# The end of a bias stage: merged stores, an early table load, and unread matmuls ahead of the first bias

## The chip, the core and the metric

The program runs on one core of one Trainium2 chip. The metric is the device time of one execution in microseconds (us), the lower the better. Before the change the median of 3 runs is 822.11 us (817.0 to 824.08). The core's engines are called by the profile's short names: PE (TensorE matmul), DVE (VectorE), ACT (ScalarE), POOL (GpSimd) and SP (SyncE, which here issues nearly all DMA transfers). The core has 16 DMA engines.

## The reference

Attention with a bias that a small network makes of the positions, and two feed-forward stages behind it. Cut to what matters:

```python
B, H, S, D = 4, 8, 576, 64
scores = (1 / sqrt(D)) * q @ k.T                       # per batch and head
x = log1p(|i - j|) / log1p(max(i, 1))                  # per pair of positions
bias = maximum(x[..., None] @ w1 + b1, 0) @ w2         # hidden 32, one value per head
attn = softmax(scores + bias[head])
x = (attn @ v)  as rows of 512
x = (g(x @ w_in)) @ w_out                              # 512 -> 2048 -> 512, g a leaky relu
out = soft mixture of 8 experts over x                 # 32 slots, experts 512 -> 1024 -> 512
```

The bias is the same for all 4 batches, so it is made once, at the start.

## The kernel before

**Stages.** The bias stage runs first (0 to about 75 us of the trace), then attention over 16 pairs of (two heads, one batch), then the feed-forward stage, then the experts. Each stage is one stream of instructions per engine, put in order when the kernel is built; instructions marked with `keep_in_program_order` keep their place, others are placed by the builder's scheduler. Once built, each engine runs its list in order, and a wait stops all that stands behind it.

**The bias stage** (`bias_phase`). The bias of one head depends on i and on |i - j|, so the kernel computes rows over the distance d = 0 to 575, in 9 steps `k` of 64 distances. In each step ACT and DVE make 16 masks (`make_mask`, L142 and L144) in a ring of `RING` buffers; PE reads all 16 for each row tile `c` (`unit`, L160); DVE combines two products into `rows` (L189, then L193 or L191); POOL writes the mirror image into the same tile (L211). The rows are split into row tiles c = 0 to 3 (two blocks of 64 positions each, one per half of the 128 partitions) and c = 4 (the middle block). Step k has the tiles c = 3 down to 0 as far as k <= 8 - c, and c = 4 for k < 5.

**Pieces and stores.** `CHUNKS[c]` cuts the steps of a row tile into pieces. A piece collects its steps in one SBUF tile `rows{c}_{i}`; with its last step it is sent to a scratch tensor in DRAM, `W` for c < 4 and `W4` for c = 4 (`send`, L216). Each half of the partitions goes out in DMAs of its own, 64 partitions each. The SBUF tiles are named by `TAGS`, one letter per piece; pieces with the same letter share a buffer, and the later one waits until the earlier one's stores have landed. With the last pieces only the first of four head pairs is sent at once (`flush(slice(0, 1))`), the other three at the very end (`late`).

**The first bias.** Attention reads the bias of a head pair back from `W` and `W4` into the tile `nb` (L345). For the first pair this goes in four parts: `att.bias_first(s)` for s = 0 to 3, part s needing row tile c = 3 - s, and the c = 4 block with s = 0. On SP the stores of the steps k > 4 and these loads stand in written order: the stores of step 6, then part 0, then the stores of step 7, part 1, the stores of step 8, parts 2 and 3, then the late stores. Behind them come the loads of the next pairs: `raw` (L365, q and k), `v` (L371), `wide` (L655, a weight of the feed-forward stage) and `nb` of the next head pair. SP hands its DMAs eight semaphores in turn, so a DMA is not issued before the one eight places ahead of it has landed.

**Attention's start.** Per pair and tile t: `scores` (S, PE L414) into PSUM, `least` (z, DVE L437: adds the bias, keeps the minimum), `power` (e, ACT L457: exp), `transposes` (T, PE L477), `gather` (g, L491 or L493), `pv` (P, PE L505). Nine tiles make a pair. The scores' PSUM pool has 4 buffers, so S of the tiles 0 to 3 of pair 0 can run before any bias is there, and S of tile 4 waits for z of tile 0. POOL splits q and k of each pair into high and low parts (L382, L384), two pairs ahead; between two of these splits the builder has put the first block of the feed-forward input (L633 to L635), which needs pair 0's result written to DRAM (`xT`, L518) and read back (`xu`, `xb`, L618, L622).

Of the kernel before, what the change touches and what calls it, by code (L numbers as in the profile page):

```python
# [13 lines left out]
AF = mybir.ActivationFunctionType  # L14
# [5 lines left out]
P = 128  # L20
# [15 lines left out]
NG = 9  # L36
NTQ = S // 4
PITCH = 2 * S
RING = 40
ACC = 4  # L40
CHUNKS = ((0, 2, 4, 7, 9), (0, 2, 4, 6, 8), (0, 3, 5, 7), (0, 2, 4, 6), (0, 2, 4, 5))
TAGS = ("cfgc", "becb", "gbd", "ada", "mnm")
LATE, EARLY = "bcdg", "aefmn"
ENGS = (
    "VVVAVVAVVAVVAVVA", "AAAVAAAVAAAVAAAV", "AAAVAAAVAAAVAAAV", "AAAVAAAVAAAVAAAV", "AAAVAAAVAAAVAAAV", "AAVAAVAAVAAVAAVA",
    "AAVAAVAAVAAVAAVA", "AVAAVAVAAVAVAAVA", "AVAVAVAAVAVAVAVA",
# [23 lines left out]
def bias_phase(tc, ident, W, W4, cpack, lcol, prow, xmain, xtail, att):  # L70


    nc = tc.nc
    with ExitStack() as ctx:
# [25 lines left out]
        sg = cp.tile([P, 4], F32, name="sg")  # L100
# [31 lines left out]

        mask = mp.tile([P, RING, S], BF16, name="mask")

        def make_mask(k, u):

            t = 16 * k + u
            n = min(S, 128 * (NG - k))
            dst = mask[:, t % RING, :n]
            on = ENGS[k][u]  # L140
            if on == "A":
                nc.scalar.activation(dst, pr[:, :n], AF.Sigmoid, bias=wb[:, t : t + 1], scale=BIG)  # L142
            else:
                nc.vector.tensor_scalar(dst, pr[:, :n], wl[:, t : t + 1], None, ALU.is_gt)  # L144
# [3 lines left out]
        def unit(k, c):  # L148
# [9 lines left out]
            for u in range(16):  # L158
                for part in range(3):
                    nc.tensor.matmul(  # L160
                        dst[:, u // 8, :, :, 4 * (u % 8) : 4 * (u % 8) + 4],
                        mask[:, (16 * k + u) % RING, cols],
                        wp[:, part],
# [3 lines left out]
            if c == 4 and k in (0, 2):  # L167
                return
            ks = CHUNKS[c]
            i = max(n for n in range(len(ks)) if ks[n] <= k)  # L170
# [6 lines left out]
            if f0 == 0:  # L177
                tag = TAGS[c][i]
                rows[c] = fps[tag].tile([P, H * 2 * w], F32, tag=tag, name=f"rows{c}_{i}")
# [84 lines left out]
        for k in range(NG):  # L264
            cs = [c for c in range(3, -1, -1) if k <= NG - 1 - c]
            if k < 5:
                cs.append(4)
            done = 0
            for n_, c in enumerate(cs):
                unit(k, c)  # L270
                if k + 1 < NG:
                    upto = 16 * (n_ + 1) // len(cs)
                    for u in range(done, upto):
                        make_mask(k + 1, u)
                    done = upto
            if k < 4:
                att.split(0, k)
            if k in (6, 7):
                att.bias_first(k - 6)
        att.load(1)  # L280
        att.load_v(1)
        att.bias_first(2)
# [5 lines left out]
class Attention:  # L288
# [107 lines left out]
    def scores(self, i, t):  # L396
        nc, st = self.nc, self.st[i]
        slot = self.SLOT[t]
        if slot == 0:
            st["sum"] = self.op.tile([P, 9], F32, tag="sum", name=f"sum{i}")  # L400
        s = self.ps.tile([P, 2, 512], F32, tag="p", name=f"s{i}_{t}")
        if slot < 4:
            terms = [(P * slot, 0)]
        elif slot == 4:
            terms = [(512, 0), (576, 1)]
        else:
            terms = [(704 + P * (slot - 5), 1)]
        seq = [(o, h, a, b) for o, h in terms for a, b in ((0, 0), (0, 1), (1, 0))]
        for n_, (o, h, a, b) in enumerate(seq):
            for hf in range(2):  # L410
                d = slice(64 * hf, 64 * hf + 64)
                self.pin(
                    i,
                    nc.tensor.matmul(  # L414
                        s[:, hf, :288],
                        st["q", a][d, o : o + P],
                        st["k", b][d, 288 * h : 288 * h + 288],
                        start=n_ == 0,
                        stop=n_ == len(seq) - 1,
                    ),  # L420
                )
        st["s", t] = s
# [738 lines left out]
def kernel(  # L1161
# [17 lines left out]
        for n, b in (("a_raw", 2), ("a_v", 3), ("a_split", 2))  # L1179
    )  # L1180
    bias_phase(tc, ident, W, W4, cpack, lcol, prow, xmain, xtail, att)

    kp = ctx.enter_context(tc.tile_pool(name="m_keep", bufs=1, reuse_waits="tile"))
# [167 lines left out]
```

## Time and profile before

| | before |
|---|---|
| median of 3 runs | 822.11 us |
| lowest and highest | 817.0 and 824.08 us |
| the profiled execution | 819.86 us |
| its span, first to last instruction | 817.8 us |
| mean granted TensorE clock in it | 0.974 of 2.4 GHz |

The span is what the trace covers; 2.06 us of the profiled execution lie around it. The views used below: busy time of each engine in chosen stretches, each engine's instructions in order of time with what ended its idle time, the chain of waits that ended last, and the DMA's traffic. A granted clock of 1.00 is 2.4 GHz and 0.50 is 1.2 GHz.

### The profile page before, as it was taken

What the parts mean: (1) busy time and instruction counts of PE and PEld (TensorE: products, weight loads), DVE (VectorE), ACT (ScalarE), POOL (GpSimd) and SP (SyncE); (2) the same over time, 40 slices, a digit from 0 to 9 for tenths busy, and PEclk for the clock granted to TensorE, in tenths of its full rate; (3) what the DMA queues carried; (4) which work ended last, traced back from release to release, by engine and by line L of the source; (5) the groups of instructions that cost most, each with busy time, mean ns of one, the idle gap of its engine ahead of it and who ended that gap; (6) DMA issues with size and microseconds to landing.
All of it is one profiled execution on the core that took longest, in us unless ns stands there. A gap on an engine that the chain in (4) does not pass through costs nothing.

```text
span 817.8 us, 18364 instructions
## 1 busy us (share of the span) xinstructions
PE 769.4 (94%) x7428; PEld 641.0 (78%) x7428; DVE 549.2 (67%) x958; ACT 495.7 (61%) x974; POOL 316.5 (39%) x239
## 2 busy tenths in 40 slices
PE   6886898999999999999999999999999999998993
PEld 6785776787877779988898889888999898885432
DVE  8896686888898866777668465646675756565003
ACT  8973786888888854443447566656666656554002
POOL 4632137365475712113224463454444451231000
PEclk9999798999999999999999999999999999998997
DMA  6599987729743442332330011301100134338996
GB/s 197 132 228 218 306 200 211 218 92 256 236 135 129 145 152 81 126 103 103 132 101 1 1 40 40 129 1 41 37 1 20 30 129 130 99 107 303 382 372 231
DMA packets 49669, 114.44 MB, mean 140 GB/s; under 512 B 10544, under 2 KB 29872, under 8 KB 47536
## 3 DMA queue, kind: packets, MB, share of 16 engines
q1 hardware_dynamic: 49584, 113.26, 44.5%
q8 instruction: 58, 0.95, 0.5%
q14 instruction: 27, 0.22, 0.1%
HBM read 91.95 MB, written 21.29 MB: 138 GB/s over the span
## 4 chain that ended last, share of the span: by engine, by line
PE 79%; DVE 6%; DMA 5%; issue 3%; POOL 3%; ACT 2%; SPq 1%; DVEq 0%; POOLq 0%; ACTq 0%
PE h L724 23%; PE ys L756 22%; PE o L505 9%; PE s L414 8%; PE t L477 4%; PE acc L160 4%; PE ops L1125 3%; PE hps L1125 2%; DMA xT<-xo 2%; DMA W<-rows 2%; DVE mask L144 1%; PE lp L816 1%; DMA em<-in_mw_dram 1%; SPq L345 1%; DVE rows L193 1%
## 5 line engine op out<-in xcount | busy, mean ns | idle before, releaser
L735 DVE SCALAR_TENSOR_TENSOR g<-g,nal 128x384 f32<-128x384 f32 x96 | 100.0, 1041 | 82.3 <-ACT g L734 82.2
L437 DVE CUSTOM_DVE_ANT_0 z<-s,nb 128x576 f32<-128x576 f32 x144 | 108.2, 755 | 24.5 <-PE s L414 14.0
L457 ACT ACTIVATE e<-z,m 128x576 f32<-128x576 f32 x144 | 109.9, 767 | 6.8 <-DVE m L437 6.8
L742 ACT ACTIVATE gr<-g 128x384 fp32r<-128x384 f32 x95 | 49.7, 523 | 86.3 <-DVE g L735 86.2
L493 ACT ACTIVATE g<-t 128x640 f32<-128x640 f32 x96 | 67.3, 703 | 35.4 <-PE t L477 31.4
L505 PE MATMUL o<-g,v 128*64 128x256 f32 (+1 forms) x640 | 86.3, 415 | 0.5 <-ACT g L493 0.5
L732 ACT ACTIVATE g<-h 128x384 f32<-128x384 f32 x96 | 46.9, 489 | 54.3 <-PE h L724 51.9
L744 DVE TENSOR_TENSOR gr<-g,gr 128x384 fp32r<-128x384 f32 x79 | 53.4, 677 | 33.7 <-ACT gr L742 30.4
L477 PE MATMUL t<-ident,e 64*128 64x64 f32 x1440 | 69.9, 227 | 3.8 <-DVE m L437 2.8
L477 PEld LDWEIGHTS t<-ident,e 64*128 64x128 f32 x1440 | 67.7, 143 | 5.3 <-issue 4.1
L160 PE MATMUL acc<-wp,mask 128*128 128x64 bf16 (+1 forms) x1680 | 57.2, 198 | 14.8 <-DVE rows L193 6.0
L160 PEld LDWEIGHTS <-mask 128*128 128x128 bf16 (+1 forms) x1680 | 55.1, 103 | 16.8 <-DVE rows L193 6.6
L414 PE MATMUL s<-kh,qh 64*128 64x288 f32 x320 | 62.5, 386 | 5.8 <-DVE m L437 4.0
L505 PEld LDWEIGHTS o<-g,v 128*64 128x64 f32 x640 | 43.8, 138 | 29.0 <-ACT g L493 1.0
L142 ACT ACTIVATE mask<-pr,wb 128x576 bf16<-128x576 f16 (+4 forms) x94 | 54.8, 678 | 6.3 <-PE acc L160 6.2
L414 PE MATMUL s<-kl,qh 64*128 64x288 f32 x320 | 49.1, 302 | 2.7 <-POOL kl L384 2.7
L744 POOL TENSOR_TENSOR gr<-g,gr 128x384 fp32r<-128x384 f32 x16 | 19.7, 1231 | 78.1 <-ACT gr L742 68.2
L414 PE MATMUL s<-kh,ql 64*128 64x288 f32 x320 | 49.1, 302 | 0.0
L382 POOL TENSOR_SCALAR qh<-raw 128x1216 fp32r<-128x1216 f32 x16 | 19.3, 1209 | 74.6 <-PE t L477 38.9
L734 ACT ACTIVATE g<-h 128x384 f32<-128x384 f32 x96 | 46.5, 485 | 0.0
L384 POOL TENSOR_TENSOR ql<-raw,qh 128x1216 fp32r<-128x1216 f32 x16 | 45.2, 2827 | 0.0
L414 PEld LDWEIGHTS s<-kh,qh 64*128 64x128 f32 x320 | 31.7, 194 | 14.9 <-DVE m L437 4.7
(986 smaller groups left out, 2020.2 us busy)
## 6 DMA issues: line engine op xcount, KB each, us to landing
wide<-in_w_dram SPq DMA_DIRECT2D x16, 1024.0 KB
ep<-in_mw_dram SPq DMA_DIRECT2D x30, 512.0 KB
raw<-in_qk_dram SPq DMA_DIRECT2D x16, 896.0 KB
nb<-W SPq DMA_DIRECT2D x6, 1152.0 KB
v<-in_v_l_dram SPq DMA_DIRECT2D x16, 320.0 KB
pre<-in_mw_dram SPq DMA_DIRECT2D x10, 512.0 KB
er<-in_mw_dram SPq DMA_DIRECT2D x9, 512.0 KB
em<-in_mw_dram SPq DMA_DIRECT2D x8, 512.0 KB
```

Source lines behind the costliest of these rows:

```text
L142: nc.scalar.activation(dst, pr[:, :n], AF.Sigmoid, bias=wb[:, t : t + 1], scale=BIG)
L160: nc.tensor.matmul(dst[:, u // 8, :, :, 4 * (u % 8) : 4 * (u % 8) + 4], mask[:, (16 * k + u) % RING, cols], wp[:, part], start=part == 0, ...
L414: nc.tensor.matmul(s[:, hf, :288], st["q", a][d, o : o + P], st["k", b][d, 288 * h : 288 * h + 288], start=n_ == 0, stop=n_ == len(seq) - 1,),
L437: self.nc.vector.tensor_tensor_reduce(out=z.rearrange("p (a b) -> p a b", a=2), in0=s[:, :, :288], in1=nb.rearrange("p (a b) -> p a b", a= ...
L457: self.nc.scalar.activation(e, z, AF.Exp, bias=m, scale=-1.0, accum_out=st["sum"][:, slot : slot + 1]),
L477: self.pin(i, nc.tensor.transpose(tp[:, r, 64 * c : 64 * c + 64], e[q, k0 : k0 + P], self.ident[q, q]))
L493: self.pin(i, nc.scalar.activation(dst, src, AF.Copy))
L505: nc.tensor.matmul(op[64 * h : 64 * h + 64, 0, :n], st["v"][:, h, c], g[:, h, c], start=c == 0, stop=c == 4),
L724: nc.tensor.matmul(h, w_[:, c * P : (c + 1) * P], x_[:, c], start=c == 0 and n_ == 0, stop=c == NC - 1 and n_ == 2,)
L735: nc.vector.scalar_tensor_tensor(g, neg, self.nal[:, f : f + 1], g, ALU.mult, ALU.add)
L744: eng.tensor_tensor(gl, g, gh.bitcast(F32), ALU.subtract)
L756: i = self.nc.tensor.matmul(self.ys[blk][t], g_[:, t * P : (t + 1) * P], w_[:, 512:], start=f == 0 and n_ == 0, stop=f == NF - 1 and n_ == 2,)
```

## The change

Four edits, all at or for the end of the bias stage.

1. **Pieces.** Row tile c = 1 goes out in three pieces (steps 0-1, 2-5, 6-7) instead of four (0-1, 2-3, 4-5, 6-7); row tile c = 3 in two (0-3, 4-5) instead of three (0-1, 2-3, 4-5). The letters change with it: the piece of steps 5-6 of c = 2 takes the letter f instead of d, and the letter f belongs to the piece of steps 2-3 of c = 0.
2. **Ring.** The ring of masks has 32 buffers instead of 40.
3. **Table.** One exp of a single column is run on ACT behind the last mask, so that the table of exponentials is loaded there.
4. **Matmuls.** 14 matmuls of 512 columns stand on PE ahead of the scores of tile 3 of pair 0, into the buffer of that tile; the scores then overwrite it.

```diff
-RING = 40
+RING = 32
 ACC = 4
-CHUNKS = ((0, 2, 4, 7, 9), (0, 2, 4, 6, 8), (0, 3, 5, 7), (0, 2, 4, 6), (0, 2, 4, 5))
-TAGS = ("cfgc", "becb", "gbd", "ada", "mnm")
-LATE, EARLY = "bcdg", "aefmn"
+CHUNKS = ((0, 2, 4, 7, 9), (0, 2, 6, 8), (0, 3, 5, 7), (0, 4, 6), (0, 2, 4, 5))
+TAGS = ("cfgc", "beb", "gbf", "ad", "mnm")
+LATE, EARLY = "bcfg", "ademn"
+WARM = 14
@@ bias_phase
             if k in (6, 7):
                 att.bias_first(k - 6)
+        tc.keep_in_program_order(nc.scalar.activation(sg[:, 3:4], ident[:, :1], AF.Exp))
         att.load(1)
@@ Attention.scores
+        if i == 0 and t == 3:
+            for _ in range(WARM):
+                self.tc.keep_in_program_order(
+                    nc.tensor.matmul(s[:, 0], st["q", 0][:, :P], st["k", 0][:, :512], start=True, stop=True)
+                )
```

How the built programs differ. First SP, the start of its stores (`rows3_0_207` is the first piece of row tile 3, the last number only counts; the shape is partitions x head pairs x float columns, so 64x4x510 are runs of 2,040 bytes in DRAM). Before:

```order
L216 DMA W_57<-rows3_0_207 64x4x510 x2
L216 DMA W4_58<-rows4_0_720 64x8x64 x2
L216 DMA W_57<-rows1_0_321 64x4x510 x2
L216 DMA W_57<-rows0_0_378 64x4x382 x2
L216 DMA W4_58<-rows4_0_720 64x8x63
L216 DMA W4_58<-rows4_0_720 64x8x64
L216 DMA W_57<-rows2_0_264 64x4x766 x2
L216 DMA W_57<-rows3_1_783 64x4x256 x4
L216 DMA W_57<-rows1_1_898 64x4x256 x2
L216 DMA W4_58<-rows4_1_1300 64x8x64
L216 DMA W_57<-rows0_1_955 64x4x256 x2
```

And SP in the changed program, the same place:

```order
L217 DMA W4_58<-rows4_0_718 64x8x64 x2
L217 DMA W_57<-rows1_0_321 64x4x510 x2
L217 DMA W_57<-rows0_0_378 64x4x382 x2
L217 DMA W4_58<-rows4_0_718 64x8x63
L217 DMA W4_58<-rows4_0_718 64x8x64
L217 DMA W_57<-rows2_0_264 64x4x766 x2
L217 DMA W_57<-rows3_0_207 64x4x1022 x2
L217 DMA W4_58<-rows4_1_1293 64x8x64
L217 DMA W_57<-rows0_1_952 64x4x256 x2
```

The stores of c = 3 that stood first (2 of 510 KB) are gone from there; where its second piece stood (4 of 256 KB), the merged piece now stands (2 of 1,022 KB, runs of 4,088 bytes). The two stores of `rows1_1` have left this place; they come as 2 of 512 KB (runs of 2,048 bytes) where 2 of 256 KB of `rows1_2` stood, just ahead of the stores of step 6. SP issues six DMAs fewer, with the same bytes.

Second DVE, in step 5, with the semaphores that each instruction waits for (DMAHW0 to 7 are SP's eight in turn). Before, the last piece of c = 2:

```order
L189 TENSOR_TENSOR tmp5_1_1769<-acc5_1_1720,xm_t_102 128x512 [waits DVE_49,PE_49]
L144 TENSOR_SCALAR mask_128<-pr_100,wl_98 128x256 [waits PE_49,Activation_49] x2
L193 TENSOR_TENSOR rows2_2_1711<-tmp5_2_1712,acc5_2_1662 128x4x2x64 [waits DMAHW5_49,DMAHW6_49,DMAHW0_49,DMAHW7_49,DVE_49,Pool_49]
L144 TENSOR_SCALAR mask_128<-pr_100,wl_98 128x256 [waits PE_49,Activation_49]
L144 TENSOR_SCALAR mask_128<-pr_100,wl_98 128x128 [waits PE_49,Activation_49]
```

And in the changed program:

```order
L190 TENSOR_TENSOR tmp5_1_1761<-acc5_1_1712,xm_t_102 128x512 [waits DVE_49,PE_49]
L145 TENSOR_SCALAR mask_128<-pr_100,wl_98 128x256 [waits PE_49,Activation_49] x3
L194 TENSOR_TENSOR rows2_2_1703<-tmp5_2_1704,acc5_2_1654 128x4x2x64 [waits DMAHW6_49,DMAHW7_49,DVE_49,Pool_49]
L145 TENSOR_SCALAR mask_128<-pr_100,wl_98 128x256 [waits PE_49,Activation_49]
L145 TENSOR_SCALAR mask_128<-pr_100,wl_98 128x256 [waits PE_49]
```

Before, this row waited for the four stores of `rows3_1`; now for the two of `rows0_1` (the semaphores 6 and 7), which stand behind the merged piece in SP's list. Masks of steps 6 to 8 that stood ahead of such rows have moved down by a place or two.

Third PE, the scores of the first pair (`s0_3` is tile 3 of pair 0; x2 is one matmul per head of the pair), in the changed program:

```order
L421 MATMUL s0_2_2270<-kh0_1013,qh0_439 128x288 x2
L421 MATMUL s0_2_2270<-kl0_1014,qh0_439 128x288 x2
L421 MATMUL s0_2_2270<-kh0_1013,ql0_440 128x288 x2
L413 MATMUL s0_3_2284<-kh0_1013,qh0_439 128x512 x14
L421 MATMUL s0_3_2284<-kh0_1013,qh0_439 128x288 x2
L421 MATMUL s0_3_2284<-kl0_1014,qh0_439 128x288 x2
L421 MATMUL s0_3_2284<-kh0_1013,ql0_440 128x288 x2
L421 MATMUL s0_4_2310<-kh0_1013,qh0_439 128x288 x2
```

Only the row of 14 is new. On ACT the table load and the one-column exp stand right behind the last mask, ahead of the first e. POOL's list is unchanged; in the last stage a few instructions of PE, DVE and ACT have changed places with a neighbour.

## Rows read from the trace of the kernel before

**Rows 1.** The page's fourth part: the chain that ended last, by line

```profile
PE h L724 23%; PE ys L756 22%; PE o L505 9%; PE s L414 8%; PE t L477 4%; PE acc L160 4%; PE ops L1125 3%; PE hps L1125 2%; DMA xT<-xo 2%; DMA W<-rows 2%; DVE mask L144 1%; PE lp L816 1%; DMA em<-in_mw_dram 1%; SPq L345 1%; DVE rows L193 1%
```

**Rows 2.** Stretches: busy us of PE, PEld, DVE, ACT, POOL; clock, DMA share, GB/s

```profile
26.00:31.00 5.00, 2.84 (x95) 2.72 (x95) 5.00 (x5) 5.00 (x8) 4.86 (x5) 1.00 0.81 199
31.00:33.00 2.00, 2.00 (x51) 2.00 (x48) 2.00 (x5) 2.00 (x4) 1.06 (x2) 0.62 0.12 37
...
44.00:50.00 6.00, 5.37 (x175) 5.09 (x173) 5.42 (x12) 6.00 (x12) 3.09 (x5) 1.00 0.94 221
...
52.00:56.00 4.00, 3.27 (x100) 3.05 (x96) 4.00 (x10) 3.71 (x9) 1.35 (x2) 1.00 0.96 242
56.00:70.00 14.00, 11.68 (x383) 11.35 (x383) 13.78 (x29) 4.96 (x14) 6.22 (x10) 1.00 0.99 230
70.00:72.00 2.00, 1.69 (x52) 1.57 (x52) 1.50 (x3) 0.00 (x0) 0.39 (x1) 1.00 0.83 222
72.00:74.00 2.00, 1.10 (x16) 1.13 (x18) 1.90 (x3) 0.00 (x0) 1.35 (x2) 1.00 0.26 57
74.00:92.00 18.00, 10.43 (x108) 9.04 (x106) 8.21 (x23) 9.40 (x21) 0.67 (x1) 0.65 0.95 250
92.00:100.00 8.00, 7.15 (x108) 5.80 (x108) 5.42 (x14) 5.61 (x12) 1.80 (x2) 0.94 1.01 353
100.00:118.00 18.00, 18.00 (x254) 13.56 (x252) 14.28 (x36) 15.44 (x35) 10.23 (x7) 1.00 1.00 245
```

**Rows 3.** DMA traffic of 44 to 50 us: packets by size

```profile
DMA packets 637, 1.33 MB, mean 221 GB/s; under 512 B 225, under 2 KB 225, under 8 KB 636
```

**Rows 4.** SP in order of time: start, duration, line, transfer

```profile
47.61 23.94 SPq L216 DMA_DIRECT2D W<-rows  x23
71.61 3.71 SPq L345 DMA_DIRECT2D nb<-W  x4
```

**Rows 5.** SP, one store by itself

```profile
57.59 0.80 SPq L216 DMA_DIRECT2D W<-rows  x1
```

**Rows 6.** The chain in order of time, 40 to 80 us: start, duration, what

```profile
50.21 4.88 DMA W<-rows
...
69.10 1.30 POOL rows L211 x2
70.41 0.50 SPq L216
```

**Rows 7.** DVE in order of time; in brackets idle before and what ended it

```profile
61.29 0.67 DVE L193 TENSOR_TENSOR rows<-tmp,acc 128x512 f32<-128x512 f32 x1
...
78.04 0.76 DVE L437 CUSTOM_DVE_ANT_0 z<-s,nb 128x576 f32<-128x576 f32 x1 [3.96 <-DMA nb<-W]
...
82.19 0.76 DVE L437 CUSTOM_DVE_ANT_0 z<-s,nb 128x576 f32<-128x576 f32 x1 [2.70 <-DMA nb<-W]
```

**Rows 8.** PE in order of time

```profile
78.86 0.40 PE L414 MATMUL s<-kh,qh 64*128 64x288 f32 x2 [3.98 <-DVE m L437]
...
83.10 0.80 PE L477 MATMUL t<-ident,e 64*128 64x64 f32 x10 [2.47 <-DVE m L437]
```

**Rows 9.** ACT in order of time

```profile
60.09 3.57 ACT L142 ACTIVATE mask<-pr,wb 128x256 bf16<-128x256 f16 x10 [4.38 <-PE acc L160]
...
78.88 1.28 ACT L457 ACT_TABLE_LOAD   x1 [12.05 <-DMA W<-rows]
```

**Rows 10.** Stretches of 2 us while the clock is low

```profile
80.00:82.00 2.00, 0.63 (x6) 0.28 (x4) 0.00 (x0) 1.78 (x5) 0.00 (x0) 0.50 1.03 271
...
90.00:92.00 2.00, 2.00 (x30) 1.99 (x28) 0.96 (x4) 1.13 (x3) 0.00 (x0) 0.50 0.82 189
```

**Rows 11.** The chain in order of time, 100 to 128 us

```profile
105.22 15.96 DMA xT<-xo
```

**Rows 12.** POOL in order of time

```profile
125.36 1.03 POOL L633 TENSOR_TENSOR xu<-xu,xb 128x384 f32<-128x384 f32 x1 [11.97 <-DMA rs<-rt]
```

**Rows 13.** PE in order of time

```profile
134.47 0.61 PE L414 MATMUL s<-kl,qh 64*128 64x288 f32 x2 [2.65 <-POOL kl L384]
```

## The prediction

> **What bounds the kernel now.** I read the page's chain first: it is mostly PE in the feed-forward stage, which the change doesn't touch; of what the change is near, only "DMA W<-rows", "SPq L345" and the bias stage's DVE lines stand in it, with 1 or 2% each [rows 1]. 1% of the span is 8.2 us, and about 1% is also what a measurement of this kernel can tell from no change, with three runs between 817.0 and 824.1 us. So the question is what a few microseconds around 30 to 134 us do.
>
> Next the stretches. In each row the reader should compare the DMA share with the engines' busy time. From 44 to 70 us the 16 DMA engines are busy 0.94 to 0.99 of the time at 221 to 242 GB/s [rows 2], and SP issues stores back to back for 23.94 us from 47.61 on [rows 4]: the stores of the bias rows are the queue. Before that there is slack: 31 to 33 us shows a share of 0.12 [rows 2]. The only hole behind it is 70 to 74 us, with 0.83 and 0.26, that is 2 x 0.17 + 2 x 0.74 = 1.8 us of idle DMA [rows 2]. It is where POOL ends the rows of step 6 (69.10 + 1.30), SP sends their small stores at 70.41 and then the first bias loads at 71.61 [rows 4, 6]. From 74 us on the DMA is full again, through 118 us (0.95, 1.01, 1.00) [rows 2].
>
> The first z waits for the first bias until 78.04, the third for part 1 until 82.19 [rows 7]. PE idles 3.98 us before 78.86 and 2.47 us before 83.10 [rows 8]; its clock is at 0.50 (1.2 GHz) from 80 to 92 us [rows 10].
>
> Last, where this stretch hands its time on. Pair 0's result is issued for DRAM at 105.22 and lands 15.96 us later, behind loads already in the queue [rows 11]. POOL waits 11.97 us for what is read back from it, until 125.36 [rows 12], and only then splits the next pair, for which PE waits 2.65 us until 134.47 [rows 13]. So the time at which PE runs on behind 134.47 is set by the DMA stream that begins with the first bias load near 74 us, and not by how fast PE was before it. A later start of that stream moves the end one for one; a PE that is faster between 79 and 131 us only waits longer here.
>
> **The change, part by part.**
>
> *The moved piece of c = 3.* Two stores of 510 KB, 1.04 MB, left when DMA had nothing else: 26 to 31 us carries 1.00 MB at 199 GB/s, and the DMA runs dry behind it [rows 2]. Now they go out with step 3, where the stores of the second piece stood, in the full stretch. At the 221 GB/s of 44 to 50 us that is 1.04 MB / 221 GB/s = 4.7 us more work in a full queue; at 242 GB/s it is 4.3, at 199 it is 5.2.
>
> *The merging.* 4,088-byte runs don't occur in the trace, so their rate is bounded by the nearest rows. 44 to 50 us is mostly runs of 3,064 bytes (of 637 packets 412 are over 2 KB) [rows 3] and reaches 221 GB/s; 52 to 56 us, runs of 1,024 bytes, reaches 242; 26 to 31 us, runs of 2,040, reaches 199 [rows 2]. Longer runs are thus not faster here. What was 1,024-byte runs in the full stretch (the second piece of c = 3 and the two middle ones of c = 1, 2.1 MB) would take 2.1 / 221 = 9.5 us instead of 2.1 / 242 = 8.7: +0.8. Worst is 199 GB/s: 10.5, +1.8. Best is 353 GB/s, the fastest stretch near (92 to 100 us, loads) [rows 2]: 5.9, -2.8, and then the moved piece costs 2.9 instead of 4.7. I take 221, the row of the same kind of store that is nearest in length. The six issues saved cost SP about 0.6 to 1 us each (23.94 / 23) [rows 4], hidden while the DMA is full; without that cover they would be worth 3.6 us at most, inside the lower bound below.
>
> All these stores leave 64 partitions. The Trainium skill, SBUF — State Buffer, section "Door 1: The DMA port swizzle", says that a transfer from 64 partitions reaches 8 of 16 ports and so about half the bandwidth, whatever else it does. The trace agrees: the stores' 199 to 242 GB/s stand against 353 GB/s where loads to 128 partitions run [rows 2]. By that rule longer runs bring nothing and the sum is the one I take.
>
> *The hole at 70 to 74 us.* With 4.7 + 0.8 = 5.5 us more work, the DMA still has stores when SP issues the small ones, so the 1.8 us of idling goes. The stores that end near 72.2 us (74.0 - 1.8) end at 77.7, and the bias loads follow at once, instead of at 74.0: **+3.7 us**.
>
> *The compute must not be later than that.* DVE's last piece of c = 2 is written from 61.29 [rows 7]. Its buffer now waits for the two stores of the second piece of c = 0; the later one was issued at 57.59, for 0.80 us, to 58.39 [rows 5]. A store in this stretch lands 4.88 us after its issue [rows 6]: 63.3. Ahead of it stand now the moved piece and half of the merging (4.7 + 0.4), but no longer the c = 1 stores (0.52 MB / 242 = 2.2): +2.9, so 66.2. DVE stands 4.9 us at this row, and with it everything behind it on DVE: rows of the steps 5 to 8, so POOL's mirror images and SP's stores. POOL's end of step 6 goes from 70.40 to 75.3, SP's first bias issue from 71.61 to 76.5. That is still ahead of 77.7, so it adds nothing to the 3.7; it does mean that a faster DMA than I think takes both away together.
>
> *Ring.* ACT already waits 4.38 us for a mask buffer before 60.09 [rows 9]; with 32 such waits come earlier and more often. Masks are wanted only when PE comes to their step, and DVE now stands for a store. I take 0; without that cover one wait like the 4.38 would be felt for the part that PE can't hide, at most 1 us (PE is busy 11.7 of 14 us from 56 to 70 [rows 2], so a late mask first uses up 2.3 us of idle).
>
> *Table.* The load of 1.28 us at 78.88 [rows 9] leaves e of tile 0. But the next PE work, the transposes at 83.10, waits for DVE's third z, which waits for part 1 of the bias until 82.19 [rows 7, 8]. Gain 0; with the bias there at once it would be 1.28.
>
> *The 14 matmuls.* L756 has 512 columns too: 22% of 817.8 us over 864 matmuls (6 blocks, 16 steps, 9 each) is 0.208 us each at 2.4 GHz [rows 1], so 14 take 2.9 us, 5.8 at 1.2 GHz. They start behind the scores of tile 2, near 74.2, inside the idle 3.98 us [rows 8], and hold up only the scores of tile 3, wanted at 83. Cost 0, 2.9 if the bias came 3 us sooner against PE. The clock is low behind that idle time [rows 8, 10]. It may fall later now, but the second gap of 2.47 us, which waits for part 1 of the bias, stands as before between the 14 and the work of 83 to 92 us [rows 8]. If the clock stayed up all the same, half of PE's 10.43 us from 74 to 92 us [rows 2] could be saved, 5.2 at most, and the wait before 134.47 would grow by as much.
>
> *Last stage.* A few neighbours change places: 0, give or take 0.5.
>
> Sum for the profiled execution: 819.86 + 3.7 = 823.6 us. The median of the runs is 2.25 us above the profiled one, so 822.11 + 3.7 = **825.8 us**. Bounds: with 353 GB/s everywhere 2.9 - 2.8 = 0.1 of added work, and at best the hole closed by fewer issues, -1.8; with 199 GB/s and the hole kept 5.2 + 1.8 = 7.0. So 820.3 to 829.1.
>
> **The rivals.**
>
> *Hidden after all.* The bias loads start at 74 as before, 822.1 us (820.6 to 823.6). It decides if the merged stores run above about 300 GB/s. For it: rates in the full stretch do swing, 221 to 353 [rows 2]. Against it: no stretch of stores exceeds 242.
>
> *Faster.* The hole closes because SP reaches the first bias load with fewer issues, and DVE's rows no longer stand behind older stores: -1.8 us, and up to 2 us more if the low clock also goes and the wait at 134.47 passes it on; 818 to 820 us. It needs the long runs to move faster than the short ones. The Trainium skill, Perfetto Trace Analysis, section "DMA Optimizations", says that DMAs under 2 KB carry much overhead and larger ones raise throughput; by that the time would be this rival's. Rows 2 speak against it.
>
> *DVE's new wait spreads.* The row at 61.29 stands longer than 4.9 us and PE's clock falls in the bias stage too: +6 to +9 us, 828 to 831. It decides if the merged piece takes over 12 us.
>
> **Numbers.** Forecast (+1.5 to +6) 0.58, hidden 0.24, faster 0.12, spread 0.06. Forecast and hidden together hold 0.82, so the range is 820.5 to 829. Faster by over 1% (below 813.9) isn't reached by a case: 0.03. Slower by over 1% (above 830.3) is the far end of the last: 0.06. Within 1%: 0.91.
>
> **What the new profile would show.** Right: DMA share near 0 from 20 to 32 us and no hole of 1.8 us before the first bias load; a DVE wait of 3 to 5 us on a store near 62 us; the first z near 81.7; the wait for POOL's split still there, PE running on near 138. Wrong: the first z at or before 78, or that PE wait gone. A merged stretch above 300 GB/s would be the step that failed.

## The result and the profile after

The changed kernel takes 823.87 us (median of 17 runs, 819.65 to 828.0); the kernel before, run beside it, 819.87 (17 runs, 814.99 to 824.08). The ratio is 1.0054, with a 95% interval of 1.0037 to 1.0070: 4.4 us slower (the two medians differ by 4.0), where +3.7 was forecast.

| | before | after |
|---|---|---|
| median beside each other | 819.87 us | 823.87 us |
| the profiled execution | 819.86 us | 822.61 us |
| its span | 817.8 us | 820.8 us |
| first bias load issued (SP, nb) | 71.61 us | 77.78 us |
| first z (DVE) | 78.04 us | 83.20 us |
| POOL continues with xu | 125.36 us | 129.34 us |
| PE runs on behind POOL's split | 134.47 us | 138.43 us |

The stretches of the changed kernel, to be laid beside [rows 2] (columns: window, its length, busy us of PE, PEld, DVE, ACT and POOL with instruction counts, granted clock, DMA share, GB/s):

```profile
26.00:31.00 5.00, 3.35 (x116) 3.23 (x112) 5.00 (x7) 5.00 (x8) 4.53 (x5) 1.00 0.02 5
...
50.00:52.00 2.00, 1.64 (x52) 1.49 (x49) 2.00 (x5) 2.00 (x5) 0.67 (x1) 1.00 0.98 289
52.00:56.00 4.00, 2.71 (x86) 2.55 (x83) 4.00 (x9) 3.60 (x8) 1.40 (x3) 1.00 0.97 261
56.00:70.00 14.00, 10.49 (x277) 10.40 (x278) 8.06 (x17) 4.95 (x13) 3.16 (x5) 0.76 0.95 221
...
74.00:76.00 2.00, 0.77 (x27) 0.77 (x27) 2.00 (x4) 0.00 (x0) 1.28 (x2) 1.00 0.69 177
76.00:78.00 2.00, 1.23 (x36) 1.14 (x34) 2.00 (x4) 0.00 (x0) 0.97 (x2) 1.00 0.26 57
78.00:80.00 2.00, 2.00 (x22) 1.70 (x19) 0.83 (x2) 0.00 (x0) 1.00 (x2) 1.00 0.62 113
```

The first store of c = 3 is gone from 26 to 31 us, as foreseen. But the hole ahead of the first bias load is still there, from 74 to 80 us: 2 x 0.31 + 2 x 0.74 + 2 x 0.38 = 2.9 us of idle DMA. And from 56 to 70 us DVE is busy 8.06 us where it was 13.78, with a clock of 0.76 where it was 1.00. Something stopped the compute. The chain of waits says what the first bias load stood behind (start, duration, what):

```profile
74.64 1.29 POOL rows L212 x2
...
75.95 0.45 SPq L217
...
76.44 1.28 SPq L217
...
77.78 0.59 SPq L347
```

It is the chain of [rows 6], 69.10 and 70.41 there, 5.5 us later: the rows of step 6 were late, not the DMA. DVE in order of time (in brackets the idle time before and what ended it), against [rows 7]:

```profile
61.42 0.69 DVE L190 TENSOR_TENSOR tmp<-acc,xm_t 128x512 f32<-128x512 f32 x1 [5.04 <-PE acc L161]
64.80 0.69 DVE L190 TENSOR_TENSOR tmp<-acc,xm_t 128x512 f32<-128x512 f32 x1 [0.90 <-PE acc L161]
83.20 0.76 DVE L444 CUSTOM_DVE_ANT_0 z<-s,nb 128x576 f32<-128x576 f32 x1 [4.34 <-PE s L421]
```

DVE waits 5.04 us for PE. (The first z is put down to the scores "PE s", but PE had begun the scores of this tile at 77.69; what came last was then the bias load, as in [rows 7].) And PE, against [rows 13] and the two lines of before that follow:

```profile
53.82 0.89 PE L161 MATMUL acc<-wp,mask 128*128 128x64 bf16 x25
59.45 0.77 PE L161 MATMUL acc<-wp,mask 128*128 128x64 bf16 x11 [4.74 <-issue]
...
75.23 1.69 PE L161 MATMUL acc<-wp,mask 128*128 128x64 bf16 x52 [1.96 <-issue]
...
138.43 0.40 PE L421 MATMUL s<-kl,qh 64*128 64x288 f32 x2 [3.24 <-POOL kl L386]
```

PE of before, the same two places:

```profile
56.84 3.91 PE L160 MATMUL acc<-wp,mask 128*128 128x64 bf16 x128 [1.57 <-DVE rows L193]
...
70.31 1.69 PE L160 MATMUL acc<-wp,mask 128*128 128x64 bf16 x52 [0.65 <-issue]
```

In the changed kernel PE stands still for 4.74 us with "issue" as the reason: no wait that the profile shows. Two views name the cause. First, how many instructions PE had begun by then, in both kernels (windows from 0; a matmul and its weight load are two instructions, and each instruction is a record of the trace):

Before:

```profile
0.00:56.00 56.00, 43.85 (x1245) 42.18 (x1245) 48.09 (x91) 52.93 (x84) 28.11 (x42) 0.97 0.68 182
0.00:70.00 70.00, 55.53 (x1628) 53.53 (x1628) 61.87 (x119) 57.89 (x98) 34.33 (x52) 0.98 0.75 192
```

After:

```profile
0.00:57.00 57.00, 43.14 (x1245) 41.55 (x1245) 48.87 (x90) 51.14 (x79) 29.50 (x44) 0.97 0.62 170
0.00:74.00 74.00, 56.90 (x1628) 55.09 (x1628) 60.55 (x117) 59.47 (x100) 33.46 (x50) 0.93 0.69 181
```

1,245 matmuls and 1,245 weight loads, with 7 drain and semaphore records that the view doesn't count as busy, make 2,497; 2 x 1,628 and 9 such records make 3,265. The difference is 768 = 3 x 256. Both kernels stand at the same two counts, before for 1.57 and 0.65 us, after for 4.74 and 1.96. Second, the DMA traffic of after around the first stand, in the two windows 48.5 to 57.1 and 57.1 to 57.2 us (queue, kind: packets, MB, share):

```profile
q1 hardware_dynamic: 612, 2.19, 95.9%
...
q1 hardware_dynamic: 4, 0.02, 82.8%
q8 instruction: 1, 0.02, 60.0%
```

A packet of 16 KB of kind "instruction" on queue 8 (256 records of 64 bytes would be that) starts at 57.15 us, takes 0.96, and PE goes on 1.34 us behind its end. In before the same packet starts at 54.45. PE had begun the block of 256 ahead of it at 51.02 us in before and 50.48 in after, so the packet came 3.4 and 6.7 us behind that, and a block keeps PE busy for some 4.2. The trace doesn't say whose instructions a packet holds. But the page of before counts 58 such packets, and PE's 7,428 matmuls and 7,428 weight loads are 58.0 times 256; the other engines' busy instructions are 239 to 974 each:

```profile
q8 instruction: 58, 0.95, 0.5%
```

So PE's instructions seem to come through the same DMA engines as the stores, and what is queued there holds them back. This is read from the trace; the experiments below test it. One rival stands at 2,497: there the instruction also waits for a semaphore of DVE, and in before the row that the profile names ended at 56.48, only 0.36 us ahead of PE. At 3,265 there is no such wait.

### The profile page after: what moved, and what is told of

It is laid out like the page before. It is cut to its first block, busy times and chain, and to the rows that moved or that the text cites. A ratio compares the mean times of both kernels' runs of the same rounds, so it can differ in the third digit from the quotient of the medians.

```text
span 820.8 us, 18387 instructions
## 1 busy us (share of the span) xinstructions
PE 771.3 (94%) x7442; PEld 642.4 (78%) x7442; DVE 549.1 (67%) x958; ACT 495.4 (60%) x975; POOL 316.5 (39%) x239
## 4 chain that ended last, share of the span: by engine, by line
PE 74%; DMA 5%; DVE 4%; issue 3%; POOL 2%; ACT 1%; SPq 1%; DVEq 0%; POOLq 0%; ACTq 0%
PE h L731 23%; PE ys L763 22%; PE o L512 8%; PE s L421 8%; PE t L484 4%; PE ops L1132 3%; DMA xT<-xo 2%; PE hps L1132 2%; PE lp L823 1%; DMA em<-in_mw_dram 1%; DMA nb<-W 1%; PE o L1159 1%; DVE z L444 1%; PE turn L1141 1%; DVE x L650 0%
```

## The experiments

Three theories. **A**, on record: the moved bytes fill DMA and SP's queue until about 77 us, and the bias loads start behind them. **D**: the stores hold back PE's instruction packet, PE stands, the rows are late. **B or C**: ring, table or matmuls carry part of it, or give something back. All times below are ratios to the kernel before, run beside each.

**One part at a time.** e1_pieces keeps the pieces and the ring, e2_warm_exp the table and the matmuls, e3_c3_only and e4_c1_only one row tile's pieces each, with the ring:

```diff
 e1:  -tc.keep_in_program_order(nc.scalar.activation(sg[:, 3:4], ident[:, :1], AF.Exp))
      -for _ in range(WARM): ...            (from the changed kernel)
 e2:  +both of these                        (to the kernel before)
 e3:  -CHUNKS[3] = (0, 2, 4, 6)             (to the kernel before, RING 32, letters as changed)
      +CHUNKS[3] = (0, 4, 6)
 e4:  -CHUNKS[1] = (0, 2, 4, 6, 8)          (to the kernel before, RING 32)
      +CHUNKS[1] = (0, 2, 6, 8)
```

> The changed kernel without the exponential of one column and without the 14 unread matmuls: pieces and the ring of 32 masks alone. Theory A (on record: the pieces make the first bias late, the other two parts are worth nothing): within 1 us of the changed kernel, so 4 to 5 us above the kernel before, and the low-clock stretch after the first bias is as long as before (13.65 us near 80 to 93), since nothing keeps TensorE busy. Rival B (ring, table or matmuls carry part of the loss): 0 to 2.5 us above before. Rival C (the matmuls bring time that the pieces eat: the low stretch in after was 6.83 us, not 13.65): 1 to 3 us above the changed kernel. In all of them TensorE should stand still near 55 us, as it did for 4.74 us in the changed kernel.

> The kernel before with the exponential of one column and the 14 unread matmuls, its own pieces and its ring of 40 masks. Theory A (on record): 0, within 0.5 us of before; the first z stays near 78.0 us, the wait for POOL's split before TensorE resumes near 134 us grows by what is won ahead of it. Rival C: 1 to 3 us below before, with the wait at the split no longer than 2.65 us and TensorE resuming earlier than 134.5. Rival B: 0.5 to 1.5 us above before, the first S3 pushed behind the matmuls.

> The kernel before with one change of the pieces: the two first pieces of block column 3 become one, stored after step 3 of the loop (runs of 4,088 bytes), and the ring of 32 masks that makes room for it. Theory A, by bytes: the 1.04 MB that went in the idle stretch of 26 to 31 us join the full stretch, +3.5 to +4.5 us. Theory D (found in the trace of after): TensorE takes in its instructions in packets of 256 records; every one of its longer stands in this phase begins at a record number 256n+193 and ends 1.3 to 1.4 us behind such a packet's landing, and the long runs of this store hold the packet back: +3.5 to +5 us, with a stand of 3 us or more at record 2497, near 55 us, and the DMA idle for 2 us or more ahead of the first bias load. By A alone the DMA is full until the first bias load and the stand stays near before's 1.6 us.

> The kernel before with the other change of the pieces: the second and third pieces of block column 1 become one, stored after step 5, and the ring of 32 masks. Theory A (on record: longer runs do not move faster, up to 0.8 us worse): 0 to +1 us. Theory D: its stores come after the stand near 55 us and have runs of 2,048 bytes, so TensorE's stand at record 2497 stays near 1.6 us; the later stands (65 and 69.5 us in before, 0.8 and 0.7 us) could grow: 0 to +1.5 us. Rival (fewer stores, fewer issues on SP's queue, the last stores out sooner): -1 to 0 us.

Measured: e1 1.0050 (1.0031 to 1.0069), e2 1.0011 (0.9996 to 1.0026), e3 1.0047 (1.0026 to 1.0068), e4 1.0003 (0.9985 to 1.0022). The merged piece of c = 3, with its letters, is the whole loss, since e3 alone has it; c = 1, the ring, the table and the matmuls measure as nothing (up to 2 us isn't excluded). PE and SP of e3 in order of time:

```profile
59.69 9.34 PE L161 MATMUL acc<-wp,mask 128*128 128x64 bf16 x255 [5.01 <-issue]
...
76.84 2.51 SPq L346 DMA_DIRECT2D nb<-W  x4
```

SP of e4, its first bias loads:

```profile
72.88 3.14 SPq L346 DMA_DIRECT2D nb<-W  x4
```

SP of e2, the same:

```profile
73.49 3.42 SPq L347 DMA_DIRECT2D nb<-W  x4
```

With the piece of c = 3 there is the stand of 5 us and the late bias load; without it neither (the longest stand of e2 in this stretch is 2.19 us, that of e4 1.31). Where PE stands isn't fixed, though. e1, whose pieces are those of the changed kernel, has no stand of 4.74 us near 55 us, as was expected, but two of half that, at the counts 2,241 and 2,497. PE of e1:

```profile
52.50 5.61 PE L161 MATMUL acc<-wp,mask 128*128 128x64 bf16 x128 [2.83 <-issue]
60.82 12.99 PE L161 MATMUL acc<-wp,mask 128*128 128x64 bf16 x383 [2.70 <-issue]
```

**Is it really the instruction packet?** e6_shift puts 128 records ahead of PE's stream:

```diff
+            for _ in range(64 if k == 0 and c == 3 else 0):
+                nc.tensor.matmul(dst[:, 0, :, :, 0:4], mask[:, 0, cols], wp[:, 0], start=True, stop=True)
             for u in range(16):
```

> The changed kernel with 64 unread matmuls more (128 records on TensorE, about 2 us of it) ahead of its first one, where it has slack: every later instruction moves back by 128 records in its stream. Theory D (TensorE waits for packets of 256 records): its longer stands between 35 and 80 us again begin at record numbers 256n+193, so 128 records earlier in its own work, and end 1.3 to 1.5 us behind the landing of such a packet. Rival E (it waits for a mask, a row or an accumulator there): the stands stay at the same matmuls, which are now records 2625 and 3393. The time: within 2 us of the changed kernel, since it depends on what the packet meets in the DMA queues.

Measured: 1.0092 (1.0065 to 1.0119), some 3 us more than the changed kernel, so the time was a miss (2 us had been the bound); the place was not. PE of e6 in order of time, its stands in brackets:

```profile
55.27 5.65 PE L163 MATMUL acc<-wp,mask 128*128 128x64 bf16 x128 [4.61 <-issue]
63.12 4.04 PE L163 MATMUL acc<-wp,mask 128*64 128x64 bf16 x128 [2.19 <-issue]
```

The windows of e6 from 0 into its two first stands, with PE's counts by then:

```profile
0.00:53.00 53.00, 39.84 (x1117) 38.43 (x1118) 40.29 (x76) 45.69 (x68) 26.84 (x40) 0.96 0.56 154
0.00:62.00 62.00, 45.49 (x1245) 43.95 (x1246) 45.43 (x87) 49.28 (x76) 28.18 (x42) 0.92 0.62 168
```

1,117 + 1,118 + 6 = 2,241 and 1,245 + 1,246 + 6 = 2,497: again 256 apart and again at the same counts, now at other matmuls of the work. The lines say it directly too: x128 matmuls (with as many weight loads, 256 records) from stand to stand. Neither instruction waits for a semaphore here, and there is no stand at 2,625, where the one of 2,497 with DVE's semaphore now is. Theory D's mechanism holds; a wait for a mask or a row doesn't.

**Run length or bytes?** e5_halves and e8_quarters keep the changed kernel and cut the merged store of c = 3 in place:

```diff
 e5: +if c == 3:
     +    move(S - n_l, w - n_l + 1, n_l - 1)
     +    move(S - 1, w, n_r)
     +    return
 e8: +if c == 3:
     +    for x in range(0, n_l + n_r - 1, 128):
     +        move(S - n_l + x, w - n_l + 1 + x, min(128, n_l + n_r - 1 - x))
     +    return
```

> The changed kernel, whole, but each store of the merged piece of block column 3 is cut in two where it stands: the same bytes at the same place of SP's queue, in four stores with runs of 2,040 and 2,048 bytes in place of two with 4,088. Theory D1 (the length of the runs holds back TensorE's instruction packet): the stand at record 2497 near 55 us falls from 4.74 to 1 to 2 us, and the time to 0 to +2 us against before. Theory D2 (the packet is held back by what is queued, however it is cut): a stand or two stands of 4 to 5 us together at records 2241 and 2497, and +3.5 to +5 us. Theory A (on record, the moved bytes keep the DMA full until the first bias load): no long stand, DMA full until the first bias load at 77 us, +3.5 to +4.5 us.

> The changed kernel, whole, with the two stores of the merged piece of block column 3 cut in place into eight with runs of 1,020 and 1,024 bytes: the same bytes at the same place, in the run length that before's stores have from 52 us on, where TensorE's packets came within 2.0 to 2.3 us of being due. Theory D3 (SP can have only so many runs under way, so runs of 1 KB leave fewer bytes queued ahead of the packet): the stand near 55 us falls from 4.74 us to 1 to 2 us. If D's stand alone made the loss, 0 to +1.5 us against before; if the moved bytes alone make it (theory A), +3.5 to +4.5 us with the DMA full until a first bias load near 77 us. Theory D2 (bytes wait however cut, as with runs of 2 KB): a stand of 4 to 5 us and +4 to +5 us.

Measured: e5 1.0055 (1.0032 to 1.0077), e8 1.0059 (1.0035 to 1.0084). Runs of 2 KB change nothing: the stands of e5 at 2,241 and 2,497 are 0.64 and 4.18 us, as by D2. PE of e5 in order of time:

```profile
58.05 8.92 PE L161 MATMUL acc<-wp,mask 128*128 128x64 bf16 x255 [4.18 <-issue]
```

With runs of 1 KB PE's packet of the next block came 2.4 us behind its block's beginning (6.7 in after), and the stand at 2,497 went. That the run length did this is not shown: e1, with runs of 4 KB, has its stands split over both counts too, and this is one execution. What stood in its place in e8: one stand earlier, behind the 3,064-byte runs of c = 2; then DVE, waiting for a store at the row for the last piece of c = 2; then SP, issuing stores without a pause until the bias loads. PE of e8 in order of time:

```profile
52.88 9.35 PE L161 MATMUL acc<-wp,mask 128*128 128x64 bf16 x256 [3.13 <-issue]
```

DVE of e8, the row that waits:

```profile
64.59 0.69 DVE L194 TENSOR_TENSOR rows<-tmp,acc 128x512 f32<-128x512 f32 x1 [1.43 <-DMA W<-rows]
```

SP of e8:

```profile
58.71 18.23 SPq L217 DMA_DIRECT2D W<-rows  x17
76.99 2.51 SPq L351 DMA_DIRECT2D nb<-W  x4
```

The two stretches of e8 around the bias load (columns as above):

```profile
74.00:76.00 2.00, 0.85 (x30) 0.72 (x25) 2.00 (x4) 0.00 (x0) 0.93 (x2) 1.00 0.57 166
76.00:78.00 2.00, 1.72 (x19) 1.55 (x20) 1.42 (x3) 0.00 (x0) 1.40 (x3) 1.00 0.45 100
```

On record SP's first bias issue was to come at 76.5, behind a DVE wait of 4.9 us for a store; the wait is there with 1.43, and the issue comes at 76.99. (The 77.7 on record is something else: the time at which the bias loads fill the DMA, 74.0 in before.) But the DMA is not full up to it, with 0.57 and 0.45, so theory A holds for SP's queue at most. The rows of step 6 are done 1.4 us earlier than in after (POOL ends them at 74.54, in after at 75.93), the bias load comes only 0.8 us earlier. So where PE's stands are shorter, SP's queue sets nearly the same time, and the loss stays: PE's stands are the limit that is seen in after, but they aren't all that the moved piece costs.

**A cut by head pairs.** e10_late was to send one head pair of the merged piece at its place and three behind the first bias loads:

```diff
-            if c < 3 and (k + 1 == ks[-1] or c == 0 and i == 2):
+            if c < 3 and (k + 1 == ks[-1] or c == 0 and i == 2) or c == 3 and i == 0:
                 flush(slice(0, 1))
                 late.append(lambda: flush(slice(1, HP)))
```

> The changed kernel, whole, with the merged piece of block column 3 stored at its place for the first pair of heads alone (0.52 MB); the other three quarters (1.57 MB) go behind the first four bias loads, as other late pieces do. Both A and D expect the full stretch to end earlier, TensorE's stand near 55 us under 2 us, and the first bias load at 70 to 74 us in place of 77.8. They leave open what it brings: if the first bias sets the end (the loss is passed on from there), -1.5 to +1 us against before; if the DMA stream up to the load of xT sets it (step h on record), the 1.57 MB are only moved to behind 80 us and it stays at +3 to +6 us.

Measured: 1.0025 (1.0009 to 1.0041), half of the loss. But the edit didn't do what was meant. `send` keeps a store in written order only for the steps k > 4, and this piece ends with step 3; the builder put its three head pairs right behind the first (SP issues them at 49.12 and 50.99 us), and all 2.09 MB moved between 48 and 60 us. DMA issues of e10 from 48 to 60 us:

```profile
W<-rows SPq DMA_DIRECT2D x2, 766.5 KB
...
W<-rows SPq DMA_DIRECT2D x1, 255.5 KB
```

So e10 is a cut of the merged piece into four stores with runs of 4,088 bytes, in place, and its expectation wasn't tested. Besides, two of the late stores, of 192 KB each, now go out at 73.06 and 73.72 us, ahead of the stores of step 6. The stand at 2,497 is 1.45 us; the next packet came late, and DVE again waited at that row for a store. PE of e10, its stand of 2.29 us:

```profile
61.95 9.50 PE L161 MATMUL acc<-wp,mask 128*128 128x64 bf16 x259 [2.29 <-issue]
```

DVE of e10:

```profile
63.26 0.69 DVE L194 TENSOR_TENSOR rows<-tmp,acc 128x512 f32<-128x512 f32 x1 [2.67 <-DMA W<-rows]
```

Why half of the loss went with the bias load at 76.07, 4.5 us later than in before, is open.

**Looking for a faster kernel.** Three tries at less in the queue when PE's packets are due. e7_early sends the first step of c = 0 and c = 1 at once, into the idle DMA of 18 to 26 us (with buffers of their own for these two pieces, not shown); e9_thirds cuts the 3,064-byte runs of c = 2's first piece; e12 and e13 add the cut to e2 and to e4.

```diff
 e7:  -CHUNKS[0], CHUNKS[1] = (0, 2, 4, 7, 9), (0, 2, 4, 6, 8)
      +CHUNKS[0], CHUNKS[1] = (0, 1, 2, 4, 7, 9), (0, 1, 2, 4, 6, 8)     (RING 32)
 e9, e12, e13:
      +if c == 2:
      +    for x in range(0, n_l + n_r - 1, 128):
      +        move(S - n_l + x, w - n_l + 1 + x, min(128, n_l + n_r - 1 - x))
      +    return
```

> The kernel before with the first pieces of block columns 0 and 1 cut in two, so that what step 0 makes of them (1.04 MB) is sent at once: in before the DMA moves nothing from 18 to 26 us and is full from 33 to 72. A ring of 32 masks makes the room. By theory A the full stretch ends 4 us earlier, but the rows of step 6 are ready only at 71.6 us, so the first bias load gains nothing or, with TensorE's shorter stands (1.8, 0.6, 1.0 and 0.8 us at its packets of 256 records in before), up to 3 us: -3 to 0 us. By theory D alone the stands shrink with the fuller early and emptier late DMA: -1 to -3 us. Rival (four stores more with runs of 512 and 1,016 bytes cost the DMA what the early start brings): 0 to +2 us.

> The kernel before with one edit: the two stores of block column 2's first piece (1.57 MB, runs of 3,064 bytes, on their way from 42.8 to 52.2 us) are cut in place into six with runs of 1,016 and 1,024 bytes. Theory D3: TensorE's packet that was due at 51.0 us and began at 54.45 comes 1 to 1.5 us earlier, the stand of 1.8 us near 55 us goes, and the first bias load, held by step 6's rows at 71.6, comes up to 1.5 us earlier: -1.5 to 0 us. Theory D2 or a gain that the DMA stream behind it eats: 0, within 0.7 us. Rival (four more stores cost SP their issue time and the DMA its rate): 0 to +1.5 us.

> The kernel before with the cut of the last call (block column 2's first piece in six stores with runs of 1 KB, which measured 0.9986 with an interval of 0.9971 to 1.0001) and with the change's exponential and 14 unread matmuls (1.0011 alone, no difference). In the cut kernel TensorE is idle from 69.7 to 73.2 and from 75.7 to 78.9 us, and its granted clock is at the lower level from 74.3 to 98.2 us, 23.9 us long. If that clock is on the path, the matmuls shorten the low stretch to 10 us or less and the time is 1 to 3 us below before. If the DMA stream sets the end whatever TensorE does there: -1.2 us, as the cut alone.

> The same cut of block column 2's first piece, on the kernel with the merged second piece of block column 1 and the ring of 32 masks (1.0003 alone). If the cut's gain is real and independent of the ring and of that piece, -1.5 to -0.5 us against before, and TensorE's stand at record 2497 stays under 1 us; if what the cut measured was chance, 0 within 0.8 us.

Measured: e7 1.0029 (1.0004 to 1.0053), e9 0.9986 (0.9971 to 1.0001), e12 1.0012 (0.9993 to 1.0030), e13 1.0023 (1.0007 to 1.0039). Nothing beats the kernel before: with e12 and e13 the gain of e9 is best read as chance. e12 (+1.0 us) and e13 (+1.9) lie outside what was expected of them, and so does e7 (+2.4), expected at -3 to 0, or up to +2 by its rival. Its stores start at 21.9 us, but now c = 2's long piece is queued at 38 us, the packet of an earlier block falls into it, and PE stands 4.65 us there, with a low clock behind it. That is one execution, of 828.30 us, where the median of e7 is 821.87: it shows what can happen, not what made the 2.4 us. PE of e7:

```profile
50.80 10.07 PE L161 MATMUL acc<-wp,mask 128*128 128x64 bf16 x256 [4.65 <-issue]
```

The stretch of e7 behind it (columns as above, the clock ahead of the DMA share):

```profile
50.00:56.00 6.00, 5.20 (x107) 5.20 (x107) 0.36 (x1) 0.93 (x2) 0.37 (x1) 0.54 0.95 235
```

e12 shows what the 14 matmuls are worth. Stretches of e9, which has none:

```profile
75.00:81.00 6.00, 2.47 (x18) 1.77 (x16) 1.45 (x4) 2.11 (x4) 0.18 (x1) 0.50 0.98 242
81.00:98.00 17.00, 13.55 (x128) 11.17 (x130) 9.57 (x25) 11.28 (x27) 1.54 (x2) 0.50 0.94 301
```

The same stretches of e12, with the 14:

```profile
75.00:81.00 6.00, 5.80 (x26) 4.88 (x27) 2.77 (x7) 0.57 (x1) 1.35 (x2) 0.50 0.92 235
81.00:98.00 17.00, 13.88 (x186) 10.67 (x186) 10.74 (x30) 11.78 (x29) 0.00 (x0) 1.00 0.96 274
```

From 81 to 98 us the clock is 2.4 instead of 1.2 GHz, and the time is no better.

**All of them together.** The profiled execution of each kernel, with its time, its first bias load and POOL's xu; the ratio is that of all runs:

| kernel | c = 3 merged | ratio | profiled, us | nb issued, us | xu, us |
|---|---|---|---|---|---|
| before | no | 1 | 819.86 | 71.61 | 125.36 |
| e9_thirds | no | 0.9986 | 819.61 | 72.44 | 124.90 |
| e4_c1_only | no | 1.0003 | 818.66 | 72.88 | 123.09 |
| e2_warm_exp | no | 1.0011 | 820.79 | 73.49 | 126.11 |
| e13_thirds_c1 | no | 1.0023 | 821.67 | 73.70 | 125.34 |
| e12_thirds_warm | no | 1.0012 | 818.51 | 73.94 | 123.82 |
| e5_halves | yes | 1.0055 | 820.48 | 75.16 | 125.74 |
| e3_c3_only | yes | 1.0047 | 822.50 | 76.84 | 127.74 |
| e8_quarters | yes | 1.0059 | 822.65 | 76.99 | 129.22 |
| e1_pieces | yes | 1.0050 | 824.29 | 77.57 | 129.14 |
| after | yes | 1.0054 | 822.61 | 77.78 | 129.34 |
| e10_late | yes, cut by head pairs | 1.0025 | 819.99 | 76.07 | 124.81 |
| e7_early | no | 1.0029 | 828.30 | 77.79 | 131.63 |
| e6_shift | yes | 1.0092 | 828.17 | 81.33 | 132.24 |

The means over the six "no" at the top and the five "yes" below them: the bias load moves from 73.0 to 76.9 (+3.9 us), xu from 124.8 to 128.2 (+3.5), the ratio from 1.0006 to 1.0053 (0.0047 x 819 = +3.9 us), the profiled executions themselves from 819.9 to 822.5 (+2.7). On average most of the delay of the first bias load is passed on, and perhaps all of it. From the bias load to xu the eleven differ by up to 4 us, so a single line says little. e10 lies off it, and so does e7, whose profiled execution is 6.4 us above its median. From xu to the end all 14 take 693.3 to 696.7 us: what is lost is lost ahead of xu.

## Why the prediction was right, and where not

- **Total**: +3.7 was forecast, +4.4 measured (interval +3.0 to +5.7: 0.0037 and 0.0070 of 819.87). The absolute 825.8 came out as 823.9 because the median of the three runs shown of before lies 2.2 us above that of all 17, which include them. That the +3.7 came so near is in part luck: at the 261 and 289 GB/s that the long runs had, the terms of the sum (1.04 MB moved, 2.1 MB merged, 1.8 us of hole closed) give only +1.5 to +0.4 us, an estimate, and in after the rest came with stands of PE that the sum doesn't have.
- **The moved piece of c = 3 as the cause**: right. e3 has the whole loss.
- **The merging (+0.8)**: wrong in size. It was sized at 221 GB/s; the stretch with the long runs moved 289 and 261 GB/s. e4 shows 0 for c = 1. Below 300, so the "hidden" rival didn't come about. With it falls the argument that longer runs bring nothing because all stores leave 64 partitions: 289 is more than half of the 353 GB/s of the loads. And six issues at 0.6 to 1 us each are 3.6 to 6 us, not 3.6 at most; no run shows a gain from them.
- **The hole goes, and the loads follow the stores**: this is the step that failed as described. The hole stayed (2.9 us) and moved to 74 to 80 us; the loads waited for step 6's rows, and the first z came at 83.20, not near 81.7. In e8, where PE's stand at 2,497 is gone, SP's stores do run up to the bias loads, at 76.99, but there too the DMA had a hole ahead of them: full up to the loads it was in neither.
- **DVE's new wait on a store (4.9 us near 62)**: not in after, where DVE came to that row later than the store's landing, having waited 5.04 us for PE. It is in e8 (1.43) and e10 (2.67). Step 6's rows ended at 75.93 as against 75.3 forecast: nearly the number, by another cause, so luck.
- **What was missing**: PE's instruction packets. Before had such stands already (1.57 us ahead of 56.84, put down to a row of DVE, and 0.65 us ahead of 70.31, to "issue"). The second was enough to ask: PE idle, nothing to wait for, DMA full.
- **Ring, table, matmuls at nothing**: right (e2, e4; for the low clock e12). The prediction's reason, that what PE gains there it waits for further on, fits the unchanged time; the wait itself wasn't followed.
- **The end is set from the first bias load on**: held on average, see the table; PE ran on at 138.43 where 138 was forecast. e10 lies off it.

Left open: how far ahead of its need the packet is asked for, how the loss shares out between PE's stands and SP's queue, and e10's half.

## What to carry to other kernels

A store left in an idle stretch of the DMA in before, at no cost that shows; merged into a longer one that leaves in a full stretch it cost 4 to 5 us, in runs of 4, 2 or 1 KB (e3, e5, e8), and half of that when cut by head pairs (e10, not explained). PE, which runs through hundreds of short instructions, depends on the DMA queues for the instructions themselves: where it stands with no wait to name, count its records, look for equal distances between the stands, and look for an "instruction" packet that landed about 1.3 us ahead of its going on. After an edit read the issues in the trace before reading the time: e10's stores had not gone where the edit was to send them. And check that the profiled execution is near the median: e7's was not. Where two limits lie within a microsecond, an experiment that removes one shows the other and no gain, so look at the trace and not at the time alone.

## What the runs showed of the hardware

- PE takes in its instructions in packets of 16 KB; its stands begin at record counts that are multiples of 256 apart (2,241, 2,497, 3,265 in before, after and e6). In the traces of all 14 kernels every stand of PE over 1.5 us between 33 and 72 us begins at 1,985, 2,241, 2,497 or 2,753, and in e6 they stay at these counts when the stream is shifted by 128 records. That the packets are PE's is inferred from this and from their number, 58; the trace doesn't name their engine.
- Such a packet takes 0.96 us ahead of after's long stand (0.88 to 1.15 ahead of the stands over 1.5 us), and PE goes on 1.3 to 1.5 us behind its end. At 2,497 it began 6.7 us (runs of 4 KB, after), 6.1 us (2 KB, e5) and 2.4 us (1 KB, e8) behind the beginning of the block ahead of it; e8 had lost 3.13 us at 2,241 before, so this is no clean row of run lengths.
- A stand of 4 to 5 us was followed by 3.4 to 6.8 us at 1.2 GHz in the bias stage.
- The stretch with runs of 4,088 bytes from 64 partitions moved 289 and 261 GB/s here, that with 1,024 bytes 242 and that with 3,064 bytes 221 [rows 2]: the length of the runs alone doesn't order the rates.
